# Retention followed by two expert layers: chunks 4 to 7 of the retention take the interleaved form that the later chunks have

## Chip, cores and metric

The kernel runs on one core of one Trainium2 chip. The metric is device time in microseconds (us), the median of three runs. The kernel before takes 809.91 us (809.86 to 809.93).

## What is computed

Queries, keys and values of 4 sequences, 8 heads, 576 positions and 64 dimensions go through a retention: causal scores with a decay for each head and no softmax. The result, 2304 tokens by 512, goes through two feed-forward layers of width 2048.

```python
scores = scale * np.matmul(q, k.transpose(0, 1, 3, 2))
Dmat = np.where(rel >= 0, gamma[:, None, None] ** rel[None, :, :], 0.0)
attn_out = np.matmul(scores * Dmat[None, :, :, :], v)
...
h = np.maximum(x @ w_in, 0.0)            # first layer
x = h * h @ w_out
h = x @ moe2_w_in                        # second layer
out = (h * np.clip(h + 3.0, 0.0, 6.0) / 6.0) @ moe2_w_out
```

## The kernel before

**The first layer sets the frame.** Its 2304 tokens are taken in five blocks of 512, 384, 512, 384 and 512. A block has 16 steps, one for each slice of 128 of the width of 2048. Step `i` issues, for TensorE, first the twelve matmuls `h` of the *next* step (`h_part`, L622), then whatever the retention puts there, then the twelve matmuls `acc` of its own step (`a_part`, L659). Every number is split into a high and a low part, so that three products stand for one. ScalarE (ACT) and VectorE (DVE) turn `h` into `g` between the two (L631, L633, L635, L641).

**In the first block the weights are prepared as well.** For each slice they are loaded as 64-bit numbers (L129, issued by SyncE, SP), scaled on ACT (L139, L140), put together on DVE (`narrow_w`, L157 and L158), cast to the high part on ACT (`cast_w`, L166), and the low part is a subtraction (`low_w`, L173): of the first-layer weight `w[f+2]` on GpSimd (POOL), of the second-layer weight on DVE. The POOL subtraction is written inside `h_part`, between the relu (L631) and the product (L633), and so stands in POOL's queue ahead of whatever the retention issues in the same step.

**The retention runs in chunks of 128 tokens.** Chunks 0 to 3 come first. The others are worked on one after the other between the steps; `retention(i)` is called between `h` and `acc` and looks up what is due. A chunk has 64x64 matmuls of four kinds: scores (k by q), totals (k by v, the update of the running state), values (probabilities by v) and reads (state by q). Around them DVE scales the keys (`scale_k`, L396), weights the scores (`weigh`, L428), scales a second copy of the queries (`scale_q`, L392), sums the states (`sum_states`, L445 and L447) and writes the low part of the result (L552); ACT writes the high part (L554). From chunk 7 on the scaling of keys and queries is POOL's (`eng`).

There are two forms of these matmuls:

- Chunks 4 to 7 (list `SCORES`, chunk 4 at step 2, then 6, 10, 13): scores and totals in one interruption of the block's matmuls (`scores`, L407 and L418), values and reads in another one two steps later (`values`, L458 and L468).
- Chunk 8 on (list `VISITS`): `visit(c)` (L495) puts scores and totals of chunk `c` and values and reads of chunk `c - 1` into one interruption, drawn alternately from the upper and the lower 64 rows. It takes the two PSUM banks of tile `at` and one of the two banks of tile `h`, called `alone` here. The scores of the lower rows and the totals of the upper rows write the same bank. So the first of those totals waits for a memset of one column on POOL (L519), which itself waits for the last score matmul:

```python
if (i, n) == (0, 0):
    relay = nc.gpsimd.memset(nothing, 0.0).ins
    after(relay, shared[-1])
...
if (i, n, e) == (0, 0, 0):
    after(ins, relay)
```

Every engine works through its own queue in the order in which the program is written, which is fixed by hand (`manual_schedule`).

Of the kernel before, what the change touches and what calls it, by code (L numbers as in the profile page):

```python
# [11 lines left out]
F32 = mybir.dt.float32  # L12
# [7 lines left out]
P = 128  # L20
# [4 lines left out]
NPAIR = H // 2  # L25
# [22 lines left out]
BT = P // 2  # L48
# [37 lines left out]
def retention_moe_kernel(ctx: ExitStack, tc, qk, kv, w1, w2, cst, out):  # L86
# [5 lines left out]
    nc = tc.nc  # L92
    nblk = len(BLOCKS)
    start = np.concatenate([[0], np.cumsum([n for n, _ in BLOCKS])]).tolist()
# [20 lines left out]
    ps_at = pool(psum, "ps_at", 1, space=bass.MemoryType.PSUM)  # L115
# [80 lines left out]
    n0 = BLOCKS[0][0] // P  # L196
    ch = {}
# [37 lines left out]
    def load_qk(c):  # L235

        if c < NCHUNK:
            t = apool.tile([P, 2, NPAIR, P], F32, tag="q", name=f"q_{c}")
            k = apool.tile([P, DM], F32, tag="k", name=f"k_{c}")
            nc.sync.dma_start(k, kv[c, :, 0])  # L240
            nc.sync.dma_start(t, qk[c].rearrange("p x (n t) -> p x n t", n=NPAIR))
            ch[c] = [t[:, 0], t[:, 1], k]

    def load_v(c):

        if c < NCHUNK:
            v = apool.tile([P, DM], F32, tag="v", bufs=2, name=f"v_{c}")
            nc.sync.dma_start(v, kv[c, :, 1])
            ch[c].append(v)

    def where(c):

        t0 = c * P
        return t0 % S == 0, t0 // S != (t0 + P - 1) // S, (t0 + P) % S == 0

    probs = {}
# [26 lines left out]
    os_ = {}  # L283
# [73 lines left out]
    def hb(i):  # L357
        return slice(BT * i, BT * i + BT)

    def cols(n, e):  # L360
        return slice((2 * n + e) * D, (2 * n + e + 1) * D)

    def block(n, e):
        return slice((NPAIR * e + n) * BT, (NPAIR * e + n + 1) * BT)
# [13 lines left out]
    rec = {}  # L378
    scs = {}
    qs = {}  # L380
    sums = {}

    def load_qs(c):
        t = qs[c] = apool.tile([P, H * BT], F32, tag="qs", name=f"qs_{c}")
        for i in range(2):
            for e in range(2):
                dst = t[hb(i), 256 * e : 256 * e + 256].rearrange("d (n t) -> d n t", n=NPAIR)
                src = qk[c, hb(e), 0].rearrange("d (n i t) -> i d n t", n=NPAIR, i=2)[i]
                nc.sync.dma_start(dst, src)

    def scale_q(c):
        eng(c).tensor_tensor(qs[c], qs[c], since, ALU.mult)  # L392

    def scale_k(c):
        k3 = ch[c][2].rearrange("p (h d) -> p h d", h=H)
        eng(c).tensor_tensor(k3, k3, kd.unsqueeze(2).to_broadcast([P, H, D]), ALU.mult)  # L396

    def scores(c):
        q, kt, k, v = ch[c]
        _, straddle, ends = where(c)  # L400
        at = ps_at.tile([P, 2, 512], F32, tag="at", name=f"sc_{c}")
        scs[c] = at[:, :, :256]
        sums[c] = at[:, 0, 256:], at[:, 1, 256:]
        for n in range(NPAIR):
            for e in range(2):
                for i in range(2):
                    nc.tensor.matmul(  # L407
                        at[hb(i), e, BT * n : BT * n + BT],
                        kt[hb(e), n, hb(i)],
                        q[hb(e), n, hb(i)],  # L410
                        start=True,
                        stop=True,
                    )

        for n in range(NPAIR):
            for i in range(1 if straddle else 0, 1 if ends else 2):
                for e in range(2):
                    nc.tensor.matmul(  # L418
                        at[hb(e), i, 256 + D * n : 256 + D * n + D],
                        k[hb(i), cols(n, e)],  # L420
                        v[hb(i), cols(n, e)],
                        start=True,
                        stop=True,
                    )

    def weigh(c):
        t = probs[c] = apool.tile([P, 2, NPAIR * BT], F32, tag="p", name=f"p_{c}")
        nc.vector.tensor_tensor(t, scs[c], decay, ALU.mult)  # L428

    def age_state(c):  # L430
        fresh, straddle, _ = where(c)
        if fresh or straddle:
            return
        m3, b3 = (t.rearrange("p (h d) -> p h d", h=H) for t in (middle(c), before(c)))
        nc.vector.tensor_tensor(m3, b3, gh[:BT].unsqueeze(2).to_broadcast([BT, H, D]), ALU.mult)

    def sum_states(c):
        new_state(c + 1)
        fresh, straddle, ends = where(c)
        for i in range(1 if straddle else 0, 1 if ends else 2):  # L440
            for e in range(2):
                u = sums[c][i][hb(e)].rearrange("p (n d) -> p n d", n=NPAIR)
                o = heads((before(c + 1) if i else middle(c)), e)
                if (fresh, straddle)[i]:
                    nc.vector.tensor_copy(o, u)  # L445
                else:
                    nc.vector.tensor_tensor(o, u, heads(middle(c), e), ALU.add)  # L447

    def values(c):
        v = ch[c][3]  # L450
        fresh, straddle, _ = where(c)
        at = ps_at.tile([P, 2, 512], F32, tag="at", name=f"o_{c}")
        os_[c] = at[:, 0, :256], at[:, 1, :256]
        read = [i for i in range(2) if not (fresh, straddle)[i]]
        for n in range(NPAIR):
            for i in range(2):
                for e in range(2):
                    nc.tensor.matmul(  # L458
                        at[hb(e), i, BT * n : BT * n + BT],
                        v[hb(i), cols(n, e)],  # L460
                        probs[c][hb(i), e, BT * n : BT * n + BT],
                        start=n == 0,
                        stop=n == NPAIR - 1 and i not in read,
                    )
        for n in range(NPAIR):
            for i in read:
                for e in range(2):
                    nc.tensor.matmul(  # L468
                        at[hb(e), i, BT * n : BT * n + BT],
                        rec[c][hb(i), cols(n, e)],  # L470
                        qs[c][hb(i), block(n, e)],
                        start=False,
                        stop=n == NPAIR - 1,
                    )

    small = cpool.tile([P, 2], F32, tag="small", name="small")
    con3, nothing = small[:, :1], small[:, 1:]

# [67 lines left out]
    def into_x(c, i, low):  # L546
        blk = next(b for b in range(nblk) if start[b + 1] > c * P)
        off = c * P - start[blk] + BT * i
        x = xs[0, blk][:, :, :, off : off + BT]
        o = os_[c][i].rearrange("p (n t) -> p n t", n=NPAIR)  # L550
        if low:
            nc.vector.tensor_tensor(x[:, 1], o, x[:, 0].bitcast(F32), ALU.subtract)  # L552
        else:
            nc.scalar.activation(x[:, 0], o, AF.Copy)  # L554
# [1 line left out]

    SCORES = [2, 6, 10, 13]
    VISITS = [17, 20, 24, 28, 33, 39, 45, 49, 53, 57, 61]  # L560

    def retention(i):
        for c, s in enumerate(SCORES, n0):
            if i == s - 1:
                scale_k(c)
                age_state(c)
            elif i == s:
                scores(c)
                weigh(c)
                scale_q(c)  # L570
                load_qk(c + 1)
            elif i == s + 1:
                sum_states(c)
                if c == n0 + 3:
                    load_v(c + 1)
            elif i == s + 2 and c < n0 + 3:
                values(c)
                for e in range(2):
                    into_x(c, e, False)
                for e in range(2):  # L580
                    into_x(c, e, True)
                load_v(c + 1)
                load_qs(c + 1)
        for c, s in enumerate(VISITS, n0 + 4):
            new = c < NCHUNK
            if i == s - 1 and new:
                scale_k(c)
                age_state(c)
            elif i == s:
                visit(c)  # L590
                if new:
                    load_qk(c + 1)
                into_x(c - 1, 1, False)
                into_x(c - 1, 0, False)
                if new:
                    sum_states(c)
                into_x(c - 1, 1, True)
                into_x(c - 1, 0, True)
            elif i == s + 1 and new:
                weigh(c)  # L600
                load_qs(c)
            elif i == s + 2 and new:
                load_v(c + 1)
                scale_q(c)
# [556 lines left out]
    for s in range(SUPERS):  # L1161
# [8 lines left out]
        for j in range(NJ):  # L1170
            e = j % 2
# [4 lines left out]
            for i, q in enumerate(ORDER):  # L1176
# [3 lines left out]
                for k, (u, wi, xi) in enumerate(  # L1180
# [6 lines left out]
                        start=k == 0 and q not in (2, 4, 3),  # L1187
                        stop=k == 5,
# [101 lines left out]
```

## Time and profile before

| | |
|---|---|
| median of 3 runs | 809.91 us |
| the profiled execution, its own time | 810.05 us |
| its span (first to last instruction) | 808.3 us |
| PE (TensorE) busy | 799.8 us, 99% of the span |
| DVE, ACT, POOL busy | 605.0 us (75%), 398.2 us (49%), 170.0 us (21%) |
| first block's steps 2 to 14, where the change lies | from about 42 to 118 us |

PE, PEld, DVE, ACT and POOL are the engines' rows in the profile, SP the engine that issues the transfers. Times in the rows are from the span's start. A matmul's end is modelled and overlaps the next one's start, so the length of a stretch of PE's work is read from start to start.

### The profile page before, as it was taken

The numbers are of one execution on the slowest core, as the hardware profiler recorded it, in microseconds if no ns is written. First come the engines' busy times: TensorE is split into PE (matmuls) and PEld (weight loads), VectorE is DVE, ScalarE is ACT, GpSimd is POOL, SyncE is SP. The second block draws the span as 40 slices with busy tenths as digits, with TensorE's granted clock in tenths as the row PEclk, the third lists the DMA queues.
The fourth block names the chain that finished last, engine by engine and source line by source line (L and its number), as shares of the span: only waits on it lengthen the run. The fifth ranks groups of instructions, "written<-read, shape, count | busy, mean of one in ns | idle before, by whom it ended". The sixth has DMA issues, their size and how long they took to land.

```text
span 808.3 us, 15639 instructions
## 1 busy us (share of the span) xinstructions
PE 799.8 (99%) x5876; PEld 744.6 (92%) x5876; DVE 605.0 (75%) x1110; ACT 398.2 (49%) x738; POOL 170.0 (21%) x161
## 2 busy tenths in 40 slices
PE   8999999999999999999999999999999999999997
PEld 8788889999888899998888999999999999999997
DVE  5989887878655578865557876989677987678764
ACT  1797745445343444444445543666234664335552
POOL 4412130211001011100000056500165300355300
PEclk9999999999999999999999999999999999999999
DMA  9956626778646487756458887979977979987785
GB/s 323 353 193 244 222 92 204 230 218 241 201 143 201 123 244 222 217 175 190 123 161 261 258 293 247 332 277 288 266 263 257 347 255 284 273 263 265 259 230 146
DMA packets 181899, 189.59 MB, mean 235 GB/s; under 512 B 60608, under 2 KB 135488, under 8 KB 181824
## 3 DMA queue, kind: packets, MB, share of 16 engines
q1 hardware_dynamic: 181824, 188.60, 74.8%
q8 instruction: 46, 0.75, 0.4%
q14 instruction: 29, 0.24, 0.1%
HBM read 149.76 MB, written 38.80 MB: 233 GB/s over the span
## 4 chain that ended last, share of the span: by engine, by line
PE 94%; DMA 2%; DVE 2%; ACT 1%; issue 0%; SPq 0%; POOL 0%; DVEq 0%; POOLq 0%
PE acc L659 24%; PE h L622 23%; PE z L1183 22%; PE z L1237 21%; PE at L495 2%; DMA q<-qk_dram 2%; DVE wt L157 1%; PE alone L495 0%; DVE wt L158 0%; PE sc L407 0%; ACT w L166 0%; PE o L458 0%; PE sc L418 0%; DMA out_dram<-t 0%; PE o L468 0%
## 5 line engine op out<-in xcount | busy, mean ns | idle before, releaser
L659 PE MATMUL acc<-g,w 128*128 128x512 f32 (+1 forms) x960 | 213.1, 370 | 0.4 <-ACT g L635 0.4
L622 PE MATMUL h<-x,w 128*128 128x512 f32 (+2 forms) x972 | 210.6, 365 | 0.2 <-ACT w L166 0.2
L622 PEld LDWEIGHTS h<-x,w 128*128 128x128 f32 x972 | 175.7, 188 | 22.8 <-ACT w L166 0.6
L659 PEld LDWEIGHTS acc<-g,w 128*128 128x128 f32 x960 | 173.7, 188 | 24.8 <-ACT g L635 0.8
L1183 PE MATMUL z<-xop,ring 128*128 128x384 f32 x1008 | 175.2, 334 | 0.0
L1237 PE MATMUL z<-spl,ring 128*128 128x384 f32 x1008 | 175.2, 334 | 0.0
L1183 PEld LDWEIGHTS z<-xop,ring 128*128 128x128 f32 x1008 | 174.8, 188 | 0.1
L1237 PEld LDWEIGHTS z<-spl,ring 128*128 128x128 f32 x1008 | 174.8, 188 | 0.0
L1098 POOL TENSOR_TENSOR aop<-aop,aop 128x384 f32<-128x384 f32 x96 | 107.6, 1130 | 296.8 <-DVE aop L1095 293.0
L1112 DVE TENSOR_TENSOR spl<-aop,spl 128x384 fp32r<-128x384 f32 x168 | 97.9, 610 | 22.9 <-ACT spl L1108 22.4
L1108 ACT ACTIVATE spl<-aop 128x384 fp32r<-128x384 f32 x168 | 86.0, 523 | 55.0 <-PE z L1237 51.3
L631 ACT ACTIVATE r<-h 128x512 f32<-128x512 f32 (+1 forms) x80 | 44.3, 554 | 115.4 <-PE h L622 115.3
L1092 ACT ACTIVATE aop<-held,small 128x384 f32<-128x384 f32 x72 | 44.4, 617 | 108.4 <-DVE held L1058 107.9
L633 DVE TENSOR_TENSOR r<-r,h 128x512 f32<-128x512 f32 (+1 forms) x80 | 50.5, 632 | 53.2 <-ACT r L631 52.9
L1058 DVE TENSOR_TENSOR held<-z,held 128x384 f32<-128x384 f32 x120 | 66.4, 554 | 26.4 <-PE z L1183 24.0
L635 ACT ACTIVATE g<-r 128x512 fp32r<-128x512 f32 (+1 forms) x80 | 47.2, 589 | 63.2 <-DVE r L633 63.2
L641 DVE TENSOR_TENSOR g<-r,g 128x512 fp32r<-128x512 f32 (+1 forms) x80 | 56.1, 701 | 21.0 <-ACT g L635 18.5
L1095 DVE SCALAR_TENSOR_TENSOR aop<-aop,held 128x384 f32<-128x384 f32 x72 | 49.8, 691 | 17.7 <-ACT aop L1092 16.1
L392 POOL TENSOR_TENSOR qs<-qs,con 128x512 f32<-128x512 f32 x11 | 15.0, 1361 | 135.5 <-DMA qs<-qk_dram 113.8
L749 ACT ACTIVATE uhi<-seven 128x896 fp32r<-128x896 f32 x32 | 30.6, 955 | 21.1 <-DVE seven L739 11.5
L754 DVE TENSOR_TENSOR seven<-seven,uhi 128x896 fp32r<-128x896 f32 x32 | 35.7, 1115 | 6.7 <-ACT uhi L749 6.4
L173 POOL TENSOR_TENSOR w<-wt,w 128x512 fp32r<-128x512 f32 x17 | 22.7, 1336 | 62.9 <-ACT w L166 60.2
(112 smaller groups left out, 626.0 us busy)
## 6 DMA issues: line engine op xcount, KB each, us to landing
ring<-w_out_hl SPq DMA_DIRECT2D x84, 512.0 KB, 4.8
ring<-w_in_hl SPq DMA_DIRECT2D x72, 512.0 KB, 4.8
raw<-w_dram SPq DMA_DIRECT2D x32, 512.0 KB, 7.0
uraw<-w_dram SPq DMA_DIRECT2D x64, 256.0 KB, 3.3
q<-qk_dram SPq DMA_DIRECT2D x17, 512.0 KB, 5.4
w_in_hl<-uhi SPq DMA_DIRECT2D x16, 448.0 KB, 3.6
w_in_hl<-seven SPq DMA_DIRECT2D x16, 448.0 KB, 4.6
w_out_hl<-uhi SPq DMA_DIRECT2D x16, 448.0 KB, 3.2
```

Source lines behind the costliest of these rows:

```text
L622: nc.tensor.matmul(hp[:, ts], w[:, wi, c * P : (c + 1) * P], x[:, xi, c, ts], start=k == 0, stop=k == 3 * NC - 1,)
L633: nc.vector.tensor_tensor(r, r, hp[:, :nb], ALU.mult)
L635: nc.scalar.activation(g[:, 0, :nb], r, AF.Copy)
L641: nc.vector.tensor_tensor(g[:, 1, :nb], r, g[:, 0, :nb].bitcast(F32), ALU.subtract)
L659: nc.tensor.matmul(acc[d][:, :nb], wt, g[:, gi, :nb], start=first, stop=stop)
L1058: fn(*a)
L1095: stt(f32(q, j), f32(q, j), 6.0, h, ALU.min, ALU.mult)
L1098: nc.gpsimd.tensor_tensor(f32(o, j), f32(a, j), f32(b, j), op)
L1108: act(t[:, 0, :], f32(q, k), AF.Copy)
L1112: tt(t[:, 1, :], f32(q, k), t[:, 0, :].bitcast(F32), ALU.subtract)
L1183: nc.tensor.matmul(bank[q], w[:, wi, u * P : (u + 1) * P], x[:, u, xi, :], start=k == 0 and q not in (2, 4, 3), stop=k == 5, skip_group_ch ...
L1237: nc.tensor.matmul(z[A_BANKS[q][n]][:, :HALF], w[:, k % 2, wi, P * n : P * (n + 1)], sp[:, g, :], start=k == 0 and m == 0 and q not in (2, ...
```

## The change

Chunk 4 keeps its scores and totals at step 2, in the old form. The lists become one: the visits of chunks 5, 6 and 7 stand at steps 6, 10 and 13, where their scores stood, and take over the values and reads of the chunk before. The three interruptions for values at steps 4, 8 and 12 are gone. The transfers move with them: the values `v` of chunk 5 are loaded at step 3, those of the later ones two steps after the visit before; the second copy of the queries, `qs`, of chunks 5, 6 and 7 is loaded one step after the chunk's own visit and scaled two steps after it, where it was loaded ahead of the scores and scaled right behind them. The function `values` goes.

```diff
-    def values(c):
...
-    SCORES = [2, 6, 10, 13]
-    VISITS = [17, 20, 24, 28, 33, 39, 45, 49, 53, 57, 61]
+    FIRST = 2
+    VISITS = [6, 10, 13, 17, 20, 24, 28, 33, 39, 45, 49, 53, 57, 61]
 
     def retention(i):
-        for c, s in enumerate(SCORES, n0):
-            if i == s - 1:
-                scale_k(c)
-                age_state(c)
-            elif i == s:
-                scores(c)
-                weigh(c)
-                scale_q(c)
-                load_qk(c + 1)
-            elif i == s + 1:
-                sum_states(c)
-                if c == n0 + 3:
-                    load_v(c + 1)
-            elif i == s + 2 and c < n0 + 3:
-                values(c)
-                for e in range(2):
-                    into_x(c, e, False)
-                for e in range(2):
-                    into_x(c, e, True)
-                load_v(c + 1)
-                load_qs(c + 1)
-        for c, s in enumerate(VISITS, n0 + 4):
+        if i == FIRST - 1:
+            scale_k(n0)
+            age_state(n0)
+        elif i == FIRST:
+            scores(n0)
+            weigh(n0)
+            scale_q(n0)
+            load_qk(n0 + 1)
+        elif i == FIRST + 1:
+            sum_states(n0)
+            load_v(n0 + 1)
+        for c, s in enumerate(VISITS, n0 + 1):
             new = c < NCHUNK
             if i == s - 1 and new:
                 scale_k(c)
```

Lines behind the removed function stand lower in the changed file: L495 is L468 there, L519 is L492, L552 is L525, L633 is L596, L641 is L604.

TensorE, steps 4 to 6 of the first block. Names end in the step or the chunk and a tile number (`o_4` the values of chunk 4, `at_5` and `alone_5` the banks of the visit of chunk 5). Before:

```order
L622 MATMUL h_0_0_5_661<-x_0_0_170,w_0_5_0_620 128x512 x12
L458 MATMUL o_4_688<-p_4_576,v_4_397 64x64 x16
L468 MATMUL o_4_688<-qs_4_399,state_4_404 64x64 x8
L659 MATMUL acc_0_0_0_448<-g_0_0_4_624,w_0_4_1_626 128x512 x4
...
L622 MATMUL h_0_0_7_801<-x_0_0_170,w_0_7_0_763 128x512 x12
L407 MATMUL sc_5_828<-q_5_579 64x64 x16
L418 MATMUL sc_5_828<-v_5_717,k_5_580 64x64 x16
L659 MATMUL acc_0_0_0_448<-g_0_0_6_767,w_0_6_1_769 128x512 x4
```

and now:

```order
L585 MATMUL h_0_0_5_663<-x_0_0_170,w_0_5_0_620 128x512 x12
L622 MATMUL acc_0_0_0_448<-g_0_0_4_624,w_0_4_1_626 128x512 x4
...
L585 MATMUL h_0_0_7_767<-x_0_0_170,w_0_7_0_729 128x512 x12
L468 MATMUL at_5_794<-q_5_579 64x64 x16
L468 MATMUL at_5_794<-p_4_576,v_4_397 64x64 x2
...
L468 MATMUL alone_5_795<-v_5_637,k_5_580 64x64 x2
L468 MATMUL at_5_794<-v_5_637,k_5_580 64x64 x8
L622 MATMUL acc_0_0_0_448<-g_0_0_6_733,w_0_6_1_735 128x512 x4
```

The values and reads of chunk 4 have left step 4 and lie inside the interruption of step 6, between the scores and the last totals of chunk 5.

POOL, steps 5 to 13 (`w_0_8_0` is the first-layer weight of step 8; with the semaphores that each instruction waits for). Before:

```order
L173 TENSOR_TENSOR w_0_8_0_816<-wt_0_8_0_795,w_0_8_0_816 128x512 [waits DMAHW7_49,Activation_49]
L173 TENSOR_TENSOR w_0_9_0_907<-wt_0_9_0_886,w_0_9_0_907 128x512 [waits DMAHW6_49,Activation_49]
...
L396 TENSOR_TENSOR k_7_1160<-k_7_1160,con_102 128x512 [waits DMAHW2_49,DMAHW3_49,DMAHW1_49,PE_49]
L173 TENSOR_TENSOR w_0_15_0_1349<-wt_0_15_0_1328,w_0_15_0_1349 128x512 [waits DMAHW3_49,Activation_49]
```

and now:

```order
L173 TENSOR_TENSOR w_0_8_0_782<-wt_0_8_0_761,w_0_8_0_782 128x512 [waits DMAHW0_49,Activation_49]
L492 MEMSET small_103 128x1 [waits PE_49]
L173 TENSOR_TENSOR w_0_9_0_905<-wt_0_9_0_884,w_0_9_0_905 128x512 [waits DMAHW2_49,Activation_49]
...
L173 TENSOR_TENSOR w_0_12_0_1070<-wt_0_12_0_1049,w_0_12_0_1070 128x512 [waits DMAHW6_49,Activation_49]
L492 MEMSET small_103 128x1 [waits PE_49,Pool_49]
...
L396 TENSOR_TENSOR k_7_1150<-k_7_1150,con_102 128x512 [waits DMAHW5_49,PE_49]
L173 TENSOR_TENSOR w_0_15_0_1309<-wt_0_15_0_1288,w_0_15_0_1309 128x512 [waits DMAHW7_49,Activation_49]
L492 MEMSET small_103 128x1 [waits PE_49,Pool_49]
```

Three memsets are new in POOL's queue, each right behind the weight subtraction of its step.

DVE, from the product of step 7 on (`r`) to the low part of `g` of the same step. Before:

```order
L633 TENSOR_TENSOR r_0_0_7_814<-r_0_0_7_814,h_0_0_7_801 128x512
L428 TENSOR_TENSOR p_5_861<-sc_5_828,con_102 128x512
L392 TENSOR_TENSOR qs_5_719<-qs_5_719,con_102 128x512
L641 TENSOR_TENSOR g_0_0_7_820<-r_0_0_7_814,g_0_0_7_820 128x512
```

and now:

```order
L596 TENSOR_TENSOR r_0_0_7_780<-r_0_0_7_780,h_0_0_7_767 128x512
L447 TENSOR_TENSOR state_5_634<-at_5_794,state_5_634 64x4x64 x2
L447 TENSOR_TENSOR state_6_859<-alone_5_795,state_5_634 64x4x64 x2
L525 TENSOR_TENSOR x_0_1_447<-alone_5_795,x_0_1_447 128x4x64
L525 TENSOR_TENSOR x_0_1_447<-at_5_794,x_0_1_447 128x4x64
L604 TENSOR_TENSOR g_0_0_7_786<-r_0_0_7_780,g_0_0_7_786 128x512
```

The sums of the states and the low parts of the result now follow the interruption directly; the weighting of the scores comes a step later and the scaling of the queries two steps later.

## Rows read from the trace of the kernel before

**Rows 1.** The page, part 4: the chain that ended last, by engine.

```profile
PE 94%; DMA 2%; DVE 2%; ACT 1%; issue 0%; SPq 0%; POOL 0%; DVEq 0%; POOLq 0%
```

**Rows 2.** Waits of PE, longest of seven: total us, times, longest.

```profile
PE unread L850 <- POOL early L844: 1.0, 1, 1.0
```

**Rows 3.** Timeline of PE, first block: start, length, engine, line, operation, count.

```profile
51.05 2.88 PE L622 MATMUL h<-x,w 128*128 128x512 f32 x12
...
57.80 2.88 PE L622 MATMUL h<-x,w 128*128 128x512 f32 x12
...
63.24 2.88 PE L622 MATMUL h<-x,w 128*128 128x512 f32 x12
66.05 0.69 PE L407 MATMUL sc<-q 64*64 64x64 f32 x32
...
70.00 2.88 PE L622 MATMUL h<-x,w 128*128 128x512 f32 x12
...
78.25 0.69 PE L458 MATMUL o<-p,v 64*64 64x64 f32 x32
```

**Rows 4.** Timeline of PE around the visits of chunks 12 and 14.

```profile
205.43 2.88 PE L622 MATMUL h<-x,w 128*128 128x512 f32 x12
...
213.12 2.88 PE L622 MATMUL h<-x,w 128*128 128x512 f32 x12
...
275.21 2.88 PE L622 MATMUL h<-x,w 128*128 128x512 f32 x12
...
282.89 2.88 PE L622 MATMUL h<-x,w 128*128 128x512 f32 x12
```

**Rows 5.** Timeline of PE: first scores, first totals of visit 8; totals of visit 10.

```profile
130.03 0.69 PE L495 MATMUL at<-q 64*64 64x64 f32 x32
...
131.48 0.63 PE L495 MATMUL at<-v,k 64*64 64x64 f32 x16
...
164.60 0.27 PE L495 MATMUL at<-v,k 64*64 64x64 f32 x2
```

**Rows 6.** Timeline of POOL: the memset of visit 10; brackets: idle before, releaser.

```profile
164.45 0.10 POOL L519 MEMSET small<- 128x1 f32 x1 [6.35 <-PE at L495]
```

**Rows 7.** Timeline of POOL, first block: weight subtractions, and what follows two of them.

```profile
67.99 1.42 POOL L173 TENSOR_TENSOR w<-wt,w 128x512 fp32r<-128x512 f32 x1 [4.46 <-ACT w L166]
...
79.55 1.30 POOL L173 TENSOR_TENSOR w<-wt,w 128x512 fp32r<-128x512 f32 x1 [4.14 <-ACT w L166]
...
103.95 1.30 POOL L173 TENSOR_TENSOR w<-wt,w 128x512 fp32r<-128x512 f32 x1 [4.14 <-ACT w L166]
105.20 1.05 POOL L396 TENSOR_TENSOR k<-k,con 128x512 f32<-128x512 f32 x1
111.03 1.41 POOL L173 TENSOR_TENSOR w<-wt,w 128x512 fp32r<-128x512 f32 x1 [4.78 <-ACT w L166]
112.41 1.29 POOL L392 TENSOR_TENSOR qs<-qs,con 128x512 f32<-128x512 f32 x1
```

**Rows 8.** Timeline, first block: what stands ahead of two of those subtractions.

```profile
67.28 0.64 ACT L166 ACTIVATE w<-wt 128x512 fp32r<-128x512 f32 x1 [0.39 <-DVE wt L158]
67.56 0.69 DVE L158 CUSTOM_DVE_ANT_0 wt<-raw,wt 128x1024 uint16<-128x1024 uint16 x1
...
78.36 0.60 ACT L631 ACTIVATE r<-h 128x512 f32<-128x512 f32 x1 [0.69 <-PE h L622]
...
78.85 0.62 ACT L166 ACTIVATE w<-wt 128x512 fp32r<-128x512 f32 x1
```

**Rows 9.** Timeline of DVE, first block: low parts of the result, sums of the states.

```profile
58.30 0.76 DVE L552 TENSOR_TENSOR x<-o,x 128x256 fp32r<-128x256 f32 x2 [1.76 <-ACT x L554]
...
74.27 1.78 DVE L447 TENSOR_TENSOR state<-sc,state 64x256 f32<-64x256 f32 x4
```

**Rows 10.** Timeline of SP: the four issues of one chunk's `qs`, in the first block.

```profile
79.47 3.23 SPq L389 DMA_DIRECT2D qs<-qk_dram  x4
```

**Rows 11.** Line L389 (the loads of `qs`) in the first block: issue to landing.

```profile
DMA to landing us min/median/max: 2.3/2.5/3.3
```

More of the change, by code (lines that the diff above doesn't have):

```diff
@@ L447, in sum_states @@
                     nc.vector.tensor_tensor(o, u, heads(middle(c), e), ALU.add)
-    def values(c):
[L450 to L456, printed above, removed]
-                for e in range(2):
[L458 to L466, printed above, removed]
-                for e in range(2):
[L468 to L474, printed above, removed]
     small = cpool.tile([P, 2], F32, tag="small", name="small")
@@ L554, in into_x @@
             nc.scalar.activation(x[:, 0], o, AF.Copy)
-    SCORES = [2, 6, 10, 13]
-    VISITS = [17, 20, 24, 28, 33, 39, 45, 49, 53, 57, 61]
+    FIRST = 2
+    VISITS = [6, 10, 13, 17, 20, 24, 28, 33, 39, 45, 49, 53, 57, 61]
     def retention(i):
-        for c, s in enumerate(SCORES, n0):
-            if i == s - 1:
-                scale_k(c)
-                age_state(c)
-            elif i == s:
-                scores(c)
-                weigh(c)
-                scale_q(c)
-                load_qk(c + 1)
-            elif i == s + 1:
-                sum_states(c)
-                if c == n0 + 3:
-                    load_v(c + 1)
-            elif i == s + 2 and c < n0 + 3:
-                values(c)
-                for e in range(2):
-                    into_x(c, e, False)
-                for e in range(2):
-                    into_x(c, e, True)
-                load_v(c + 1)
-                load_qs(c + 1)
-        for c, s in enumerate(VISITS, n0 + 4):
+        if i == FIRST - 1:
[10 more added lines that the diff above has]
+        for c, s in enumerate(VISITS, n0 + 1):
             new = c < NCHUNK
```

## The prediction

> **What bounds the kernel now.** I read the chain of waits first: 94% of what ended last is TensorE's own work [rows 1]. The list of PE's waits comes next: its longest is 1.0 us, on a memset of the start [rows 2], and in PE's timeline no matmul from step 3 to the end of the first block has idle time noted ahead of it [rows 3]. So in the stretch that changes, and in all that follows, the time is the sum of what PE has to issue. Less work on PE, or work in fewer pieces, shortens the kernel by as much; a wait of PE lengthens it by as much, since nothing behind it has slack in which to catch up. The timeline of PE then gives the prices, from start to start, and the timelines of POOL, ACT and DVE tell when the partners of a new wait are ready.
>
> **What is saved on PE.** An undisturbed step of the first block, from one `h` to the next, lasts 63.24 - 57.80 = 5.44 us [rows 3]. The step with the values of chunk 4 lasts 57.80 - 51.05 = 6.75, the one with the scores of chunk 5 70.00 - 63.24 = 6.76 [rows 3]. So an interruption costs 1.31 to 1.32 us. I take 1.32 for the values of chunks 5 and 6 and the scores of 6 and 7 too: each has the same 32 matmuls.
>
> A combined interruption can be read where the kernel already has it between steps of the same 512 columns. Chunk 12: 213.12 - 205.43 = 7.69, less 5.44 is 2.25 us. Chunk 14, with the chunk before it lying over a sequence border as chunk 4 does: 282.89 - 275.21 = 7.68, so 2.24 us [rows 4]. One combined interruption in place of two saves 1.31 + 1.32 - 2.24 = 0.39 us for chunks 4 and 5, and 1.32 + 1.32 - 2.25 = 0.39 us for 5 and 6 and for 6 and 7. The gain is 3 x 0.39 = **1.17 us**. The visit of chunk 8 at step 17 is what it was.
>
> **What is added: a wait for POOL.** Every visit has its first upper total wait for a memset on POOL, which waits for the last score. In the visits of the kernel before that costs nothing. The first total is due 131.48 - 130.03 = 1.45 us after the first score [rows 5], and POOL, which has been idle for 6.35 us before such a memset, is done long before [rows 6]. In the first block POOL isn't idle. The order of the changed kernel puts each of the three new memsets right behind the weight subtraction L173 of the same step, and that subtraction can't run early: it needs the cast on ACT, which stands behind the relu of the `h` that ended just as the interruption began. So the price is how late that subtraction is.
>
> - From the start of an interruption to the start of L173: 79.55 - 78.25 = 1.30 us where nothing else delays it [rows 3, 7]. There the relu starts 0.11 and the cast 0.60 after the interruption's start, as early as `h` lets them [rows 8]. This is the floor. The largest in the rows is 67.99 - 66.05 = 1.94 us, where the cast had to wait another 0.39 for DVE's L158 and ACT the rest [rows 3, 7, 8].
> - From L173's start to the next instruction of POOL: 105.20 - 103.95 = 1.25 us, or 112.41 - 111.03 = 1.38 us for one of the longer kind [rows 7].
> - From the memset's start to the total that it lets go: 164.60 - 164.45 = 0.15 us [rows 5, 6]. In that visit the total is due almost at once, so this may hold a little of PE's own work; I keep it.
>
> Less the 1.45 us that PE is busy anyway, a wait is at least 1.30 + 1.25 + 0.15 - 1.45 = 1.25 us and at most 1.94 + 1.38 + 0.15 - 1.45 = 2.02 us. PE works in order, so all its later matmuls stand behind the waiting total, the step's `acc` first.
>
> Which value? The delays of the cast in the rows belong to steps in which DVE was behind. DVE was idle for 1.76 us in each step with values, waiting for ACT's high part before its low part [rows 9]; those steps now have no such wait, so DVE comes into the visits earlier and I take 1.30 for the cast. For the subtraction I take 1.38 in the visits of chunks 5 and 6, whose steps before hold the key scaling on DVE, so that L158 runs beside the start of L173 as it does beside the 1.42 us one [rows 7, 8]; and 1.25 in that of chunk 7, where POOL scales the keys. That is 1.38 + 1.38 + 1.25 = **4.01 us** of waiting.
>
> Here the rows and a rule of the notes part. L173 took 0.12 us longer beside the DVE instruction with two SBUF inputs (1.42 against 1.30) [rows 7, 8]. The Trainium skill (SBUF — State Buffer, section "SBUF: two separate sides") says that such a DVE instruction and GpSimd hold a shared port pair one at a time, for a whole instruction, and that the loser fully blocks. By that rule a subtraction that starts just behind an L158 would be held for all of its 0.69 us and the three waits together could grow by up to 3 x (0.69 - 0.12) = 1.7 us, an estimate from the page's rule; I go by the rows.
>
> **What costs nothing, and why.** Chunk by chunk DVE and ACT do the same operations. After a visit DVE has the sums and low parts, 1.78 + 0.76 = 2.54 us [rows 9], ahead of the low part of `g`; that is needed only at the end of the next step's `acc`, and PE first has an `acc` and an `h` to issue, 5.44 us [rows 3]. If that cover were gone, PE would wait out the rest of the 2.54. The bank `alone` displaces one `h`; the next `h` goes into the other bank, which DVE's product frees during the visit and the `acc`. On SP the loads of `qs` now stand behind the visit, with two chunk loads and two weight loads ahead of them: 3.23 us of issuing [rows 10] and at most 3.3 to landing [rows 11] make 6.5, and DVE wants them two steps later, 2 x 5.44 = 10.9 us. The 4.4 us between cover the four loads ahead. If they didn't, DVE's scaling would stand in front of the low part of `g` and PE would wait in turn.
>
> **The sum.** Against the profiled execution: 810.05 - 1.17 + 4.01 = 812.89 us. The median of the runs shown is 0.14 us below that execution, so 809.91 + 2.84 = **812.75 us**.
>
> **The rivals.**
>
> - *The waits are hidden, and only the saving is left.* The memset would have to be done by the time PE comes to the totals, as in the nine visits of the kernel before. For it: POOL has long idle times ahead of every L173 (over 4 us) [rows 7]. Against it: it is idle because it waits for ACT's cast, and the cast can't precede the relu of an `h` that has just ended. Time: 809.91 - 1.17 = 808.74 us, within 0.2% of before and not slower. It decides from where the three waits together are below 1.17 + 1.62 = 2.79 us, 0.93 each (0.2% is 1.62 us, about what a measurement of this kernel tells from no change). Chance 0.07.
> - *The waits are at their upper bound.* DVE is as late in the visits as before, the cast waits for it, and each wait is 2.02 us: 809.91 - 1.17 + 6.06 = 814.8 us. For it: with the scores of chunk 5 the subtraction was that late [rows 3, 7]. Against it: the 1.76 us of idle time on DVE are gone. The port rule above leads to about the same time. Chance 0.17.
> - *A second wait behind the first.* DVE reaches the scaling of `qs` before the load has landed, or the weight loads behind a visit come late for ACT, and PE waits once more. The rows leave 4.4 us of slack; a miss of 1 us in two of three visits would give 814.8 us. Chance 0.05.
> - *Part of the wait is not lost.* Leaving the small matmuls costs PE some time in every interruption, and that may pass inside the wait. An interruption's price beyond its matmuls can't be more than a few tenths; 0.2 each would give 812.1 us. It lies inside my forecast's own range.
>
> **How the numbers follow.** The forecast, three waits of 1.25 to 1.4 us, has a chance of 0.71. Its own range is 812.0 (0.25 a visit less than the sum) to 813.2 us. The range for 8 in 10 reaches up to the second and third rival: 811.9 to 814.8 us. Slower by over 0.2% (over 811.53 us) in all cases but the first rival and a sliver of the last: 0.91. Within 0.2%: 0.08. Faster by over 0.2% would need a gain that no row shows: 0.01.
>
> **What would show it.** In the profile after, PE's interruptions at steps 4, 8 and 12 are gone and those at steps 6, 10 and 13 lengthen their steps by 3.5 to 3.65 us, where a combined one without a wait lengthens it by 2.25. PE's waits name the memset, three times, 1.2 to 1.4 us each. On POOL the memset starts 2.55 to 2.7 us after the first score, directly behind L173. DVE's 1.76 us idle times before L552 are gone. The prediction is wrong if the memsets start within 1.4 us of the first score (no wait), if PE starts the totals without them, if PE waits elsewhere in steps 7 to 16, or if a stretch after step 17 changes its length.

## Result

The changed kernel takes 816.66 us (median of six runs, 815.07 to 818.63) where the kernel before took 809.96 us (six runs, 809.86 to 810.12): 1.0086 of before, 95% interval 1.0075 to 1.0096. It is slower, by 6.7 us. Slower was forecast and the wait for POOL was its reason, but the time forecast was 812.75 us, and its range ended at 814.8. The profiled execution took 817.27 us with a span of 815.5; against that of before (810.05 and 808.3) it is 7.2 us longer. Its runs also lie further apart, 3.6 us where those of before had 0.26.

### The profile page after: what moved, and what is told of

Same layout as the page of the kernel before. It is cut to its first block, busy times and chain, and to the rows that moved or that the text cites. A ratio compares the mean times of both kernels' runs of the same rounds, so it can differ in the third digit from the quotient of the medians.

```text
span 815.5 us, 15648 instructions
## 1 busy us (share of the span) xinstructions
PE 800.9 (98%) x5876; PEld 745.6 (91%) x5876; DVE 608.6 (75%) x1110; ACT 398.2 (49%) x738; POOL 169.7 (21%) x164
## 4 chain that ended last, share of the span: by engine, by line
PE 85%; issue 8%; POOL 2%; DVE 2%; DMA 1%; ACT 1%; SPq 0%; POOLq 0%; DVEq 0%
PE z L1146 21%; PE z L1200 21%; PE acc L622 20%; PE h L585 19%; PE at L468 2%; POOL w L173 2%; DMA kv<-kv_dram 1%; DVE wt L157 1%; PE alone L468 1%; DVE wt L158 0%; DVE g L604 0%; PE sc L274 0%; PE o L291 0%; DVE w L173 0%; POOL k L396 0%
## 5 line engine op out<-in xcount | busy, mean ns | idle before, releaser
L596 DVE TENSOR_TENSOR r<-r,h 128x512 f32<-128x512 f32 (+1 forms) x80 | 50.6, 632 | 54.0 <-ACT r L594 53.6
L604 DVE TENSOR_TENSOR g<-r,g 128x512 fp32r<-128x512 f32 (+1 forms) x80 | 54.9, 686 | 21.7 <-ACT g L598 19.2
L392 POOL TENSOR_TENSOR qs<-qs,con 128x512 f32<-128x512 f32 x11 | 14.7, 1338 | 144.7 <-DMA qs<-qk_dram 134.8
L173 POOL TENSOR_TENSOR w<-wt,w 128x512 fp32r<-128x512 f32 x17 | 22.5, 1324 | 65.0 <-ACT w L166 62.3
```

Of the source, the lines that this page charges most:

```text
L596: nc.vector.tensor_tensor(r, r, hp[:, :nb], ALU.mult)
L604: nc.vector.tensor_tensor(g[:, 1, :nb], r, g[:, 0, :nb].bitcast(F32), ALU.subtract)
```

## The profile after

The waits of PE, in total, times and longest; the first row answers to [rows 2]:

```profile
PE at L468 <- POOL small L492: 5.5, 3, 2.2
...
PE acc L622 <- DVE w L173: 0.3, 1, 0.3
```

The three waits are there, and one on DVE, at step 15, in the stretch in which the prediction allowed none. The timeline of PE at the three visits (start, length, line, operation, count, and in brackets the idle time before it); it answers to [rows 3]:

```profile
64.79 0.69 PE L468 MATMUL at<-q 64*64 64x64 f32 x32
68.30 0.68 PE L468 MATMUL at<-v,k 64*64 64x64 f32 x16 [1.89 <-POOL small L492]
68.92 3.02 PE L622 MATMUL acc<-g,w 128*128 128x512 f32 x12
71.78 2.88 PE L585 MATMUL h<-x,w 128*128 128x512 f32 x12
...
90.91 0.69 PE L468 MATMUL at<-q 64*64 64x64 f32 x32
94.00 0.27 PE L468 MATMUL at<-v,k 64*64 64x64 f32 x2 [1.46 <-POOL small L492]
...
111.17 0.69 PE L468 MATMUL at<-q 64*64 64x64 f32 x32
114.99 0.27 PE L468 MATMUL at<-v,k 64*64 64x64 f32 x2 [2.19 <-POOL small L492]
...
115.84 4.33 PE L622 MATMUL acc<-g,w 128*128 128x512 f32 x12
120.01 2.88 PE L585 MATMUL h<-x,w 128*128 128x512 f32 x12
```

Without a wait the first total comes 1.45 us after the first score [rows 5]. Here it comes 3.51, 3.09 and 3.82 us after it, so the waits are 2.06, 1.64 and 2.37 us, 6.07 in sum. And the `acc` behind the third wait takes 120.01 - 115.84 = 4.17 us, the one behind the first only 71.78 - 68.92 = 2.86. The clock tells why. Busy times in stretches of that place (length, then PE, PEld, DVE, ACT, POOL, the granted clock, DMA share, GB/s):

```profile
117.00:118.00 1.00, 1.00 (x4) 0.81 (x3) 0.94 (x3) 0.00 (x0) 0.00 (x0) 0.50 0.92 291
...
120.00:121.00 1.00, 1.00 (x6) 0.83 (x5) 0.97 (x3) 0.00 (x0) 0.00 (x0) 1.00 1.02 319
```

In the profiled execution TensorE works after the third wait at a granted clock of 0.50, the lower of its two levels (1.2 GHz in place of 2.4), until about 119 us. Why the memset is late is seen on POOL, as in [rows 7]:

```profile
66.82 1.39 POOL L173 TENSOR_TENSOR w<-wt,w 128x512 fp32r<-128x512 f32 x1 [4.45 <-ACT w L166]
68.16 0.09 POOL L492 MEMSET small<- 128x1 f32 x1
...
107.03 1.29 POOL L173 TENSOR_TENSOR w<-wt,w 128x512 fp32r<-128x512 f32 x1 [4.14 <-ACT w L166]
108.27 1.51 POOL L396 TENSOR_TENSOR k<-k,con 128x512 f32<-128x512 f32 x1
113.51 1.39 POOL L173 TENSOR_TENSOR w<-wt,w 128x512 fp32r<-128x512 f32 x1 [3.73 <-ACT w L166]
114.84 0.09 POOL L492 MEMSET small<- 128x1 f32 x1
...
124.89 1.30 POOL L392 TENSOR_TENSOR qs<-qs,con 128x512 f32<-128x512 f32 x1 [9.95 <-DMA v<-kv_dram]
126.14 1.49 POOL L396 TENSOR_TENSOR k<-k,con 128x512 f32<-128x512 f32 x1
```

L173 starts 66.82 - 64.79 = 2.03 and 113.51 - 111.17 = 2.34 us after the first score (92.53 - 90.91 = 1.62 in the visit between), not the 1.30 of the floor. The floor was read in a step with values. In the steps of the kernel before that held the scores, and hold the visits now, L173 was late already; its scores and subtractions of steps 10 and 13 (the last of these subtractions, and both rows of step 6, stand in [rows 3, 7]):

```profile
90.45 0.69 PE L407 MATMUL sc<-q 64*64 64x64 f32 x32
92.08 1.42 POOL L173 TENSOR_TENSOR w<-wt,w 128x512 fp32r<-128x512 f32 x1 [4.46 <-ACT w L166]
...
109.41 0.69 PE L407 MATMUL sc<-q 64*64 64x64 f32 x32
```

There it starts 67.99 - 66.05 = 1.94, 92.08 - 90.45 = 1.63 and 111.03 - 109.41 = 1.62 us after the first score. So the first two visits have it about where it was; only the third has it later, by 0.72 us. The casts on ACT that it needs in the changed kernel, as in [rows 8]:

```profile
66.11 0.63 ACT L166 ACTIVATE w<-wt 128x512 fp32r<-128x512 f32 x1 [0.62 <-DVE wt L158]
...
91.82 0.63 ACT L166 ACTIVATE w<-wt 128x512 fp32r<-128x512 f32 x1 [0.21 <-DVE wt L158]
...
112.80 0.63 ACT L166 ACTIVATE w<-wt 128x512 fp32r<-128x512 f32 x1 [0.93 <-DVE wt L158]
```

All three wait for DVE. DVE is late at the third visit because of the step before it, and it loses time at step 15 in the same way:

```profile
107.07 1.80 DVE L392 TENSOR_TENSOR qs<-qs,con 128x512 f32<-128x512 f32 x1
108.90 1.42 DVE L435 TENSOR_TENSOR state<-state,con 64x512 f32<-64x512 f32 x1
...
116.68 0.88 DVE L447 TENSOR_TENSOR state<-at,state 64x256 f32<-64x256 f32 x2 [2.31 <-ACT x L527]
...
124.95 1.78 DVE L604 TENSOR_TENSOR g<-r,g 128x512 fp32r<-128x512 f32 x1
126.65 1.53 DVE L173 TENSOR_TENSOR w<-wt,w 128x512 fp32r<-128x512 f32 x1
```

The rows of 1.42 to 1.80 us are operations that take about 0.7 us when POOL is quiet; each overlaps one of POOL's rows at 107.03, 108.27, 124.89 and 126.14. The idle time ahead of DVE's low parts has not gone either: it now stands before the sums (2.31 us here), which wait for ACT's high part.

The account of the 7.2 us between the two profiled executions: saved by merging -1.17; three waits +6.07; the slower clock after the third wait +1.5 (1.31 in `acc`, about 0.2 in the totals); the wait for DVE's weight low part at step 15 +0.55 (127.56 to 130.87 us, 3.31, where the kernel before needs 123.67 - 120.91 = 2.76). That is 6.95; some 0.2 us, in the matmuls right behind the waits, I leave unassigned.

## Experiments

Theory A: the loss is PE's wait for a memset behind L173 in POOL's queue, and the slow stretch that such a wait brings. Rival B: the combined interruption is itself dear in the first block. Rival C: the slow stretch has nothing to do with the wait. The runs of the kernel before beside these lay at 809.83 us (809.04 to 811.25) for the first four and 809.81 us (809.28 to 810.41) for the last three.

**1. The memset ahead of L173.** In steps 6, 10 and 13 `low_w` is written behind the visit:

```diff
-            low_w(0, f + 2, (0,))
+            if f not in (6, 10, 13):
+                low_w(0, f + 2, (0,))
...
         retention(i)
+        if blk == 0 and f in (6, 10, 13):
+            low_w(0, f + 2, (0,))
```

> In steps 6, 10 and 13 the weight subtraction L173 is written behind the visit, so that POOL's memset stands ahead of it; all else as in the changed kernel. Theory A (the loss is TensorE's wait for a memset that stands behind L173, with a slow stretch of TensorE that such a wait brings): the three waits of 2.06, 1.64 and 2.37 us and the half-speed stretch go, the saving of 1.17 us stays, and so does the 0.55 us lost at step 15; 809.96 - 1.17 + 0.55 = 809.3 us, with runs as close together as those of the kernel before. Rival B (the combined interruption itself is dear in the first block, whatever POOL does): about 816 us, as the changed kernel.

Measured: 811.58 us (810.88 to 812.71), 1.0022 of before, interval 1.0013 to 1.0031. Some 5 of the 6.7 us are gone, and B falls. But it is 2.3 us above what was expected, and not faster than before. PE's waits and its timeline show a wait that stood hidden behind the other:

```profile
PE acc L622 <- DVE w L173: 1.6, 2, 1.2
```

```profile
64.09 0.69 PE L468 MATMUL at<-q 64*64 64x64 f32 x32
65.54 0.63 PE L468 MATMUL at<-v,k 64*64 64x64 f32 x16
...
71.68 0.39 PE L622 MATMUL acc<-g,w 128*128 128x512 f32 x1
72.51 2.81 PE L622 MATMUL acc<-g,w 128*128 128x512 f32 x11 [0.44 <-DVE w L173]
75.16 2.88 PE L585 MATMUL h<-x,w 128*128 128x512 f32 x12
...
115.41 0.39 PE L622 MATMUL acc<-g,w 128*128 128x512 f32 x1
117.00 2.79 PE L622 MATMUL acc<-g,w 128*128 128x512 f32 x11 [1.21 <-DVE w L173]
119.63 2.27 PE L585 MATMUL h<-x,w 128*128 128x384 f32 x12
```

The totals come 65.54 - 64.09 = 1.45 us after the scores: no wait for POOL. The `acc` of the step after, 2.72 us long elsewhere, takes 3.48, 3.08 and 4.22 us after the three visits, 2.62 us too much in sum; its second matmul needs the low part of the second-layer weight. DVE, of the third visit:

```profile
113.22 0.87 DVE L447 TENSOR_TENSOR state<-at,state 64x256 f32<-64x256 f32 x2 [1.76 <-ACT x L527]
...
116.26 0.69 DVE L173 TENSOR_TENSOR w<-wt,w 128x512 fp32r<-128x512 f32 x1
```

DVE stands idle for 1.76 us ahead of the sums, until ACT has written the high part, and the weight's low part stands behind sums and low parts. -1.17 + 2.62 = +1.45 us; measured +1.75, with 1.45 inside the interval. Its profile agrees: from the `h` of step 4 to the first `h` of the second block it takes 124.50 - 50.38 = 74.12 us, the kernel before 123.67 - 51.05 = 72.62, so 1.50 more.

**2. The memset first in step 13 alone** (the same edit with `(13,)`).

> The memset stands ahead of L173 in step 13 alone. Theory A: the waits of 2.06 and 1.64 us stay, that of 2.37 goes with the half-speed stretch that followed it in the profile; 809.96 - 1.17 + 0.55 + 3.70 = 813.0 us. If the shorter waits can bring a half-speed stretch too, up to 1.5 us more for each, and runs that spread. Rival B: about 816 us.

Measured: 814.66 us (813.53 to 815.36), ratio 1.0060, interval 1.0046 to 1.0073. The waits of 2.05 and 1.65 us are there, the third has gone, and in its profile the clock falls after neither. The expectation missed DVE once more: the `acc` of steps 14 and 15 take 1.06 and 0.57 us longer. -1.17 + 3.70 + 1.63 = +4.2 us, measured +4.8. The profiled execution is the fastest of the four; what the others lost beyond it no profile shows.

**3. The keys of chunk 7 a step earlier.**

```diff
+            if i == s - 1 - (c == n0 + 3) and new:
+                scale_k(c)
             if i == s - 1 and new:
-                scale_k(c)
                 age_state(c)
-            elif i == s:
+            if i == s:
```

> The keys of chunk 7 are scaled on POOL at step 11 instead of 12; the memsets stay behind L173. If DVE was late at step 13 because its scalings of step 12 ran beside POOL's key scaling (1.80 and 1.42 us instead of about 0.7 each), the cast at step 13 waits for DVE no longer, the wait there falls from 2.37 to about 1.5 us, and with it the half-speed stretch becomes rarer: 814.5 us without one. If DVE's own work made it late, the wait stays at 2.3 us and the time at 816.6 us.

Measured: 814.32 us (814.13 to 814.70), ratio 1.0057, interval 1.0044 to 1.0071, as expected without a slow stretch. DVE and ACT of steps 12 and 13:

```profile
107.50 1.34 DVE L392 TENSOR_TENSOR qs<-qs,con 128x512 f32<-128x512 f32 x1
108.87 0.69 DVE L435 TENSOR_TENSOR state<-state,con 64x512 f32<-64x512 f32 x1
```

```profile
112.05 0.63 ACT L166 ACTIVATE w<-wt 128x512 fp32r<-128x512 f32 x1 [0.21 <-DVE wt L158]
```

L435 is back at 0.69 us and ends at 109.56, where it ended at 110.32. L392 is not cured, though shorter: it starts later and ends at 108.84, as before, behind POOL's L173, which still runs beside it (106.99 to 108.29). The cast's wait falls from 0.93 to 0.21 us, L173 of the visit starts 112.75 - 111.13 = 1.62 us after the first score, as in the kernel before, and PE's third wait falls from 2.37 to 114.23 - 111.13 - 1.45 = 1.65 us. The clock stays at 0.999 to 1.000 in all four runs, which lie within 0.6 us of each other.

**4. The subtraction twice, so that the memset comes later.**

```diff
+            if f in (6, 10, 13):
+                w, t = wts[0, f + 2, 0]
+                nc.gpsimd.tensor_tensor(w[:, 1, :], t, w[:, 0, :].bitcast(F32), ALU.subtract)
             low_w(0, f + 2, (0,))
```

> The weight subtraction of steps 6, 10 and 13 is done twice on POOL (the second writes the same values), so that each memset comes 1.25 us later. Theory A: three waits longer by 1.25 us, 816.66 + 3.75 = 820.4 us if the half-speed stretches stay as they are, up to 823 to 824 us if now each of the three waits is followed by one. Rival C (the half-speed stretch has nothing to do with the wait): 820.4 us, and none or one such stretch, anywhere. Rival B: no change, 816.7 us.

Measured: 823.59 us (820.88 to 823.88), ratio 1.0160, interval 1.0143 to 1.0177. The three waits and the first matmuls behind them, and the clock there:

```profile
68.56 1.12 PE L468 MATMUL at<-v,k 64*64 64x64 f32 x16 [3.24 <-POOL small L492]
69.61 5.24 PE L622 MATMUL acc<-g,w 128*128 128x512 f32 x12
...
98.31 0.37 PE L468 MATMUL at<-v,k 64*64 64x64 f32 x2 [2.81 <-POOL small L492]
99.36 4.12 PE L622 MATMUL acc<-g,w 128*128 128x512 f32 x12
...
122.19 0.37 PE L468 MATMUL at<-v,k 64*64 64x64 f32 x2 [3.55 <-POOL small L492]
```

```profile
68.00:74.00 6.00, 5.44 (x26) 4.40 (x27) 3.77 (x9) 2.69 (x6) 0.51 (x2) 0.50 0.35 110
...
98.00:103.00 5.00, 4.70 (x43) 3.88 (x44) 2.69 (x7) 2.89 (x6) 0.25 (x2) 0.66 0.48 144
...
122.00:127.00 5.00, 4.82 (x44) 3.96 (x45) 2.82 (x7) 0.66 (x2) 0.13 (x2) 0.66 0.50 149
```

In the profiled execution, the slowest of the four, a slow stretch now stands behind every one of the three longer waits, and the median is the time expected for that. The fastest run, 820.88 us, has a mean clock of 0.996 where the profiled one has 0.990, so not every execution has all of them. B falls again, and C with it: the three stretches stand at the three waits.

**5. Both queues put right.** Experiment 1, and DVE does the low part of `g` and the weight's low part ahead of the sums:

```diff
-            if 1 < f:
+            if 1 < f and f - 1 not in (6, 10, 13):
                 low_w(0, f, (1,), nc.vector)
...
+        if blk == 0 and f in (6, 10, 13):
+            g_low(*steps[i + 1])
+            low_w(0, f + 1, (1,), nc.vector)
         retention(i)
...
-        if blk == 0 and i:
+        if blk == 0 and i and f not in (6, 10, 13):
             g_low(*steps[i + 1])
```

> As the first experiment (memset ahead of the weight subtraction on POOL), and in steps 6, 10 and 13 DVE does the low part of g and the low part of the second-layer weight of the next step ahead of the sums of the states instead of behind them. Theory D (what was left of the loss in the first experiment is DVE: its sums wait 1.76 us for ACT's high part of the result, and the weight's low part stands behind them, 0.7 + 0.4 + 1.5 us of waits in acc): these waits go, and the saving of 1.17 us is what remains: 809.83 - 1.17 = 808.7 us, 0.9986 of before. Rival B (the combined form costs more than the rows of the later blocks say): no better than the first experiment, 810.9 to 811.6 us.

Measured: 808.83 us (808.14 to 809.34, 11 runs), 0.9988 of before, interval 0.9979 to 0.9997. PE's longest wait is that of the start, and its `h` of step 4 and the first `h` of the second block lie closer together:

```profile
PE unread L813 <- POOL early L807: 1.0, 1, 1.0
```

```profile
50.45 2.88 PE L585 MATMUL h<-x,w 128*128 128x512 f32 x12
...
121.95 2.27 PE L585 MATMUL h<-x,w 128*128 128x384 f32 x12
```

This beats both kernels, the one before narrowly: 0.98 us less, where the rows promised 1.17. Between those two `h` the profile has 121.95 - 50.45 = 71.50 us, the kernel before 72.62: 1.12 less. The saving of the combined form was priced rightly.

**6. The same with the keys of chunk 7 early.**

> As the one before, with the keys of chunk 7 scaled on POOL at step 11 instead of 12. Theory D: PE has no wait left in steps 6 to 16 in either, so the same 808.7 us; 0.3 to 0.5 us less than the one before only if a wait at step 15 or 16 is left there.

Measured: 808.63 us (808.40 to 809.58), 0.9988, interval 0.9979 to 0.9997: the same as experiment 5. With no wait left on PE, DVE's delay at step 12 costs nothing.

**7. DVE's part alone**, the memsets still behind L173 (experiment 5 without experiment 1's edit).

> The changed kernel with DVE's two operations ahead of the sums, and the memsets still behind the weight subtractions. Theories A and D: the waits for the memset stay (6.07 us in sum, with the half-speed stretch), since they end before DVE's operations are wanted; only the 0.55 us at step 15 may go: 816.1 to 816.7 us. If DVE's order were the first cause, the time would fall to about 811 us.

Measured: 817.88 us (817.73 to 817.99), ratio 1.0101, interval 1.0087 to 1.0115. The waits for the memset are the same, 5.6 us in three, and none on DVE is left, as expected; DVE's order was not the first cause. The stretch that the edit touches behaves as expected, too: from the `h` of step 4 to the second block's first it takes 131.33 - 51.98 = 79.35 us, against 130.87 - 51.07 = 79.80 in the changed kernel. The total is 1.2 to 1.8 us above the expectation, and in the profile some 0.9 us of it come from another place, the kernel's first microseconds (the `h` of step 4 starts at 51.98 us in place of 51.07):

```profile
9.76 1.09 PE L291 MATMUL o<-p,v 128*64 128x128 f32 x16 [2.19 <-POOL v L266]
```

```profile
12.00:14.00 2.00, 2.00 (x28) 1.78 (x28) 1.18 (x2) 0.00 (x0) 1.75 (x2) 0.50 1.02 416
```

PE came to this matmul earlier than in the changed kernel, waited 2.19 us in place of 0.85, and began it 0.39 us later (9.76 against 9.37); there too the clock fell to 0.50 afterwards. Why this kernel's start differs is not shown; nothing in the edit touches it.

## Why the prediction was wrong

- **What bounds the kernel** was right: PE's issue, and any wait of PE adds to the time.
- **The saving**, 3 x 0.39 = 1.17 us: right. With all waits gone experiment 5 keeps 0.98 us, with 1.17 inside its interval, and 1.12 in its profile.
- **The wait for POOL** was right in place, cause and count: three waits, each for a memset directly behind L173. Experiment 1 removes them by the order of two instructions.
- **The size of the waits** failed in the step "DVE comes into the visits earlier and I take 1.30 for the cast". L173 starts 2.03, 1.62 and 2.34 us after the first score, so the waits sum to 6.07 us, not 4.01; the other two terms held (1.34, 1.33 and 1.33 us from L173 to the memset). The 1.30 came from a step with values. The steps that received the visits had 1.94, 1.63 and 1.62 in the kernel before, of which the prediction read only the first; with these three its own sum would have been 814.0 us. DVE did not come earlier: its rows show it without idle time ahead of the late casts, with the key scaling and the aging of the state in the step before the first two visits, and `qs` and the aging before the third. That this work is what makes the first two late is read from the rows; no run takes it away. The idle time that was to vanish moved behind the visit. For the third visit I chose the smallest wait because POOL scales those keys; it is the largest, because DVE's aging of the state stood beside that scaling and took 1.42 us. Experiment 3 shows it: keys a step earlier, L435 at 0.69, 0.72 us less of wait. The second rival, with DVE late, gave 6.06 us; that its sum fits to 0.01 is luck, for its upper bound of 2.02 a visit was passed twice and once not reached (2.06, 2.37 and 1.64).
- **The port rule** of the Trainium skill (SBUF — State Buffer, "SBUF: two separate sides") I had set against a row in which POOL lost 0.12 us, and gone by the row. For L173 itself the row was right: it took 1.38 to 1.39 us in the three visits. But POOL's L396 ends at 108.27 + 1.51 = 109.78 us; DVE's L435, noted from 108.90, ends at 110.32, 0.54 after it, where experiment 3 has it last 0.69. That nearly fits the page's sentence that the loser "fully blocks". The loser that counted was DVE, which the prediction did not look at.
- **What costs nothing** failed in one item. It gave DVE's work after a visit a cover of 5.44 us because the low part of `g` is wanted late. Behind it in DVE's queue stands the low part of the second-layer weight, wanted by the second matmul of the next `acc`, and the sums ahead of it wait 1.76 us for ACT. In the changed kernel PE's wait for POOL hid all of that (the `acc` after the first visit takes 77.22 - 74.50 = 2.72 us, as elsewhere); with that wait gone, experiment 1 pays 2.62 us. The 0.55 us at step 15 are something else, again DVE beside POOL: its low part of `g` and of the weight took 1.78 and 1.53 us while POOL scaled `qs` and keys. In experiment 3 the same two take 0.69 us each and that wait is gone. So the third rival, a second wait behind the first, came true in part, though not by the loads that it named.
- **No term for the clock.** The sum held PE's speed constant. Two of the three waits of the profiled execution left the clock at 1.00, the third brought 1.5 us at the lower level. The runs' mean clocks lie from 0.994 to 0.998, and the slowest run has the lowest; but the second slowest, the profiled one, has 0.998, so the spread is not explained by the clock alone. By the second rival's terms alone the time would have ended at 814.8 us, below every run.

## What to carry to other kernels

When work is moved to another place of the program, a cross-engine handshake that cost nothing in its old place has to be priced anew from the *queue* in which its partner will stand, and from what that queue's head waits for. After a wait is found, follow each queue past it to the first instruction that PE wants: the next wait may be hidden behind the first and appear only when that is removed. And a price is to be read in the steps that the change touches: the same wait's largest term stood in the kernel before, in the three steps that became visits. The cure was order alone: 816.66 us became 808.83 with the same instructions (the kernel before beside them took 809.96 and 809.81).

## What was not expected of the hardware

- A wait of PE costs more than its length when the clock falls after it. Idle times of 1.46 to 1.91 us, as PE's rows note them, left the granted clock at 1.00 in the profiles read here; those of 2.19 (in two kernels), 2.20, 2.81, 3.24 and 3.55 us were each followed by a stretch at 0.50. Behind the visits it cost about 1.5 us each time, and 2.6 us after the first wait of experiment 4. These are single executions: another run of the changed kernel has a mean clock of 0.994 where the profiled one, with its one slow stretch, has 0.998, and no profile shows where it was slow; so the shorter idle times are not shown to be harmless. The Trainium skill (TensorE: Matmul & The Clock Gate, "What's actually happening") says that throttled is the default state and that activity releases it, which fits these rows.
- DVE operations of 0.68 us on two SBUF inputs took 1.3 to 1.8 us when a POOL operation of 1.3 to 1.5 us ran beside them. Whenever they are noted to start, they end behind POOL's: in the changed kernel the four pairs end at 108.32 and 108.87, 109.78 and 110.32, 126.19 and 126.73, 127.63 and 128.18 us, 0.54 to 0.55 apart. POOL's key scaling grew as well, from 1.05 [rows 7] to 1.51 us.
